# The first batch's length-47 steps: from one frequency at a time to chunks of four on 64x64 tiles, joined on GpSimd

## The chip, the cores and the metric

The kernel runs on one core of a Trainium2 chip. The metric is device time in microseconds (us) of one execution, as the median of several runs. A core has TensorE (PE in the profile, with weight loads as PEld), VectorE (DVE), ScalarE (ACT), GpSimd (POOL) and SyncE (SP); the last only issues DMAs here. ScalarE and GpSimd issue DMAs as well, each in the order of its own queue.

## The reference

All data are float32, but the mixer's weights arrive as float64. There are two parts in a row: a filter in the frequency domain along the sequence, and an MLP mixer over tokens and channels.

```python
batch, seq, dim = 8, 3008, 256
X = np.fft.rfft(x, axis=1)
F = (filt_r + 1j * filt_i)[None, :, :]       # 1505 x 256
y = np.fft.irfft(X * F, n=3008, axis=1)
# mixer on y: w_tok1 (3008, 256), w_tok2 (256, 3008), w_ch1 (256, 1536), w_ch2 (1536, 256)
h = np.maximum(y.transpose(0, 2, 1) @ w_tok1, 0) @ w_tok2
u = y + h.transpose(0, 2, 1)
out = u + np.maximum(u @ w_ch1, 0) @ w_ch2
```

## The kernel before

The transform of length 3008 is split into 64 x 47. For each batch the kernel does a step of length 64 (`a_unit` or `a_pair`), then, for each of 32 frequencies k2 of that step, a step of length 47 forward, the product with the filter, and a step of length 47 back. The results go to DRAM (`g_tmp`), and are read back in another layout (`t4_load`, L778) for the mixer, which undoes the length-64 step along with its own products. `dft(bs)` (L563) is a generator that issues these steps piece by piece; the main program steps through it and puts other work between the pieces. The order of instructions on each engine is thus written out by hand; nothing is reordered by a scheduler, and each engine runs its own list in order and waits on semaphores.

The first batch is a case by itself. The results of its length-64 step stay on the chip: they are copied into `turned` and transposed in place in 32x32 blocks (L650), so that the 4 x 24 rows of one frequency lie in four groups of 32 partitions, of which 24 are used. Then, one frequency k at a time:

- `b_unit(k)` (L663): one matmul of 128x128 weights on 256 columns, into PSUM, and one VectorE product with the filter (L670, 128x512).
- `bi_unit(k)` (L673): two matmuls (L679) that accumulate the two products, and a ScalarE copy out of PSUM (L689 in `by_block`). Every second frequency's results go to `g_tmp` in one DMA on ScalarE's queue (L686).

For this, the filter rows of two frequencies are loaded into the lower 64 partitions (`filt_load`, L235, mostly on GpSimd's queue, six DMAs a pair), ScalarE copies them to the upper 64 (`filt_double`, L253), and ScalarE makes a second, swapped and negated copy of the table of weights (`table_turn`, L260 and L261).

The other batches do the same in chunks c of four frequencies, on the four 64x64 quarters of TensorE: `b_sets(c)` (eight matmuls by `four`, L525), `products(c)` (two VectorE products of 128x1024, L706), `join(c)` (two VectorE additions of 128x512, L711 and L712) and `bi_sets(c)` (eight matmuls, L525). Their products lie in the tiles `p1` and `p2`, with one buffer each (pools `p1p`, `p2p`).

Beside the first batch's length-47 steps, the main program converts the mixer's float64 weights, 16 tiles over the 32 frequencies: `convert_middle` and `convert_end` take turns, one at each step of the generator. A tile takes an ACT scaling (L281), two VectorE instructions in the middle (L283, L284), two at the end (L287, L289), and, for the first 18 tiles, two TensorE matmuls on 512 columns (L327 on the first two's result, L328 on the last two's), which `convert_middle` issues in `sum_up`, and a ScalarE copy (L330). So the matmuls of a tile stand on TensorE behind the step in which the next `convert_middle` falls. After these steps come the rest of the weights, with the sums of GpSimd (`combine`, L380 to L384), the token mixing of the first batch (`token_sums`, L783), and then the loop over the mixer's items, `mix`, with the other batches' filter steps in it. Some GpSimd additions on the weights (L801, L922) run there too.

```python
for i, _ in enumerate(dft(GROUPS[0])):
    k = i - NXC - 2
    ...
        while half < 2 * IN_B * (k + 1) // K2:
            if half % 2:
                convert_end()
            else:
                convert_middle()
            half += 1
```

Of the kernel before, what the change touches and what calls it, by code (L numbers as in the profile page):

```python
# [10 lines left out]
FP32 = mybir.dt.float32  # L11
# [48 lines left out]
def _make_tables():  # L60
# [41 lines left out]
    wbi0 = np.zeros((4, K2, K2, P + KR))  # L102
    wbi0[:, 0:A, :, 0:P] = wb
    wbi0 = wbi0.reshape(P, K2, P + KR)
    wbi0[:, :, P:] = wi
    places = np.zeros((P, K2, 2 * P))
    places[:, :, 0::2] = wbi0[:, :, 0:P]
    places[:, :, TI:TI + 2 * KR:2] = wbi0[:, :, P:]
    wbi0 = np.concatenate((places[one, :, 0:P], places[two, :, P:]))
    wbi0 = wbi0.reshape(P, K2 // WC, WC, P).transpose(0, 1, 3, 2)  # L110
    wb = wb.reshape(KR, K2, P)
    wbi = np.zeros((P, K2 // KC, 4, HALF))
    for h in range(2):
        r, to = slice(h * HALF, h * HALF + KH), slice(h * HALF, (h + 1) * HALF)
        for i in range(KC):
            wbi[r, :, i] = wb[h * KH:(h + 1) * KH, i::KC, to]
            wbi[i * HALF:(i + 1) * HALF, :, 2 + h, 0:KH] = wi[to, i::KC, h * KH:(h + 1) * KH]
    wa = wa.reshape(P, K2, 4)
# [10 lines left out]
def kernel(  # L129
# [92 lines left out]
    def filt_quad(c):  # L222
        t = filts[c % FB]
        for i, src in enumerate((filt_r, filt_i)):
            for odd in range(KC):
                k, to = c * KD + odd, odd * HALF
                nc.sync.dma_start(t[to:to + A, i], raw(src, k, [[64 * D, A], [KC * D, 2], [1, D]]))
                down = t[to + 32:to + 32 + A]
                if k:
                    nc.sync.dma_start(down[0:A - 1, i], raw(src, 64 - k, [[64 * D, A - 1], [-KC * D, 2], [1, D]]))  # L230
                else:
                    nc.sync.dma_start(down[:, i, 0], raw(src, 32, [[64 * D, A], [1, D]]))
                    nc.sync.dma_start(down[0:A - 1, i, 1], raw(src, 64 - KC, [[64 * D, A - 1], [1, D]]))

    def filt_load(c):  # L235
        t, k0 = filts_0[c % len(filts_0)], c * KC


        q = nc.gpsimd if c != 1 else nc.sync
        for src, i, p0 in ((filt_r, 0, 0), (filt_i, 1, 0)):  # L240
            q.dma_start(t[p0:p0 + A, i], raw(src, k0, [[64 * D, A], [D, KC], [1, D]]))
            lo = p0 + 32
            if k0 == 0:
                q.dma_start(t[lo:lo + A, i, 0, :], raw(src, 32, [[64 * D, A], [1, D]]))
            k = max(k0, 1)

            for j0, n in ((0, 16), (16, A - 1 - 16)):
                q.dma_start(t[lo + j0:lo + j0 + n, i, k - k0:KC, :],
                            raw(src, 64 * (j0 + 1) - k, [[64 * D, n], [-D, k0 + KC - k], [1, D]]))

    def filt_double(c):
        t = filts_0[c % len(filts_0)]
        nc.scalar.copy(out=t[HALF:P], in_=t[0:HALF])  # L253


    turn_i = sp.tile([P, 4, WC, KR], FP32, tag="s", name="turn_i")

    def table_turn(g, wb):
        wi, to = wb[:, TI:TI + 2 * KR:2].rearrange("p r k -> p k r"), turn_i[:, g % 4]
        nc.scalar.copy(out=to[0:HALF], in_=wi[HALF:P])  # L260
        nc.scalar.activation(out=to[HALF:P], in_=wi[0:HALF], func=AF.Copy, scale=-1.0)  # L261


# [299 lines left out]
    def dft(bs):  # L563
# [5 lines left out]
        kept = []  # L569

        def table_load(c):
            if first:
                if c < 5:
                    where, tag = (t1p, "t1") if c > 2 else (wbp, "wb")
                    t = where.tile([P, 2 * P, WC], FP32, tag=tag, name="wb")
                    for h in range(2):
                        nc.gpsimd.memset(t[half_of(h), ts(1 - h, P)], 0.0)
                    kept.append(t)
                wbs[c] = kept[c % 5]
                for h in range(2):  # L580
                    nc.sync.dma_start(wbs[c][half_of(h), ts(h, P)], wbi0_d[half_of(h), c])
            else:
                wbs[c] = wbp.tile([P, 2, 4, HALF], FP32, tag="wb", name="wb")
                nc.sync.dma_start(wbs[c], wbi_d[:, ts(c, 2)])
# [4 lines left out]
        def w_load(c):  # L589
            table_load(c)  # L590
            (filt_load if first else filt_quad)(c)
# [45 lines left out]
        for i, u in enumerate(() if tiled else todo):  # L637
            if first and i in (0, 2):
                w_load(i // 2)
            if first and i in (6, 8):  # L640
                table_load(i // 2 - 1)
# [9 lines left out]
        t2s, t3s, prods = {}, {}, {}  # L651
# [11 lines left out]
        def b_unit(k):  # L663
            ps = bank("pg").rearrange("p (b d) -> p b d", b=2)[:, 0:nb, :]
            nc.tensor.matmul(ps, wbs[k // WC][:, 0:2 * P:2, k % WC], turned[:, k, :].unsqueeze(1), start=True, stop=True)  # L665
            t = filts_0[k // KC % len(filts_0)]
            if k == 0:
                prods["all"] = p1p.tile([P, 2, 2, D], FP32, tag="p1", name="p1")
            p1 = prods["all"][:, k % 2]
            nc.vector.tensor_tensor(out=p1, in0=ps.to_broadcast([P, 2, D]), in1=t[:, :, k % KC, :], op=ALU.mult)  # L670
            prods[k] = (p1[:, 0:1], p1[:, 1:2])

        def bi_unit(k):  # L673


# [692 lines left out]
```

## Time and profile before

| | |
|---|---|
| median of 3 runs | 2401.42 us (2400.28 to 2402.54) |
| profiled execution | 2401.9 us, span of the trace 2400.1 us |
| busy share of the span | PE 98%, PEld 84%, DVE 81%, ACT 29%, POOL 27% |
| length-64 step of the first batch | PE 5.0 to about 20.6 us, transposes on DVE to 31.1 us |
| length-47 steps of the first batch | first TensorE matmul 31.2 us, first product 32.5 us, last product 101.8 us |
| last store to `g_tmp` of the first batch | issued at 104.7 us |
| filter issues on GpSimd | 92 of about 0.56 us |

Times in the trace count from the span's start. A row of the stretches has its bounds, its length, then the busy time of PE, PEld, DVE, ACT and POOL with the number of instructions in brackets, the granted TensorE clock, the share of the DMA engines and GB/s. A row of the timeline has start, duration, engine, line, operation, output and inputs, and in square brackets how long the engine had been idle and who ended it. Matmuls overlap in the records: two float32 records of 256 columns show 0.59 us, but take 0.43 us of the chain. A chain row has start, duration and what ran.

### The profile page before, as it was taken

The numbers are of one execution on the slowest core, as the hardware profiler recorded it, in microseconds if no ns is written. First come the engines' busy times: TensorE is split into PE (matmuls) and PEld (weight loads), VectorE is DVE, ScalarE is ACT, GpSimd is POOL, SyncE is SP. The second block draws the span as 40 slices with busy tenths as digits, with TensorE's granted clock in tenths as the row PEclk, the third lists the DMA queues.
The fourth block names the chain that finished last, engine by engine and source line by source line (L and its number), as shares of the span: only waits on it lengthen the run. The fifth ranks groups of instructions, "written<-read, shape, count | busy, mean of one in ns | idle before, by whom it ended". The sixth has DMA issues, their size and how long they took to land.

```text
span 2400.1 us, 37049 instructions
## 1 busy us (share of the span) xinstructions
PE 2361.8 (98%) x13132; PEld 2012.4 (84%) x13132; DVE 1949.6 (81%) x3669; ACT 689.8 (29%) x1339; POOL 641.6 (27%) x1124
## 2 busy tenths in 40 slices
PE   7989999999999999999999999999999999999998
PEld 4767788888898888988888888988889888898887
DVE  7798887888887888778887788788887788877786
ACT  5732222222223222232222222122222322212222
POOL 7475624211211121112111311221121112112121
PEclk8999999999999999999999999999999999999999
DMA  8864446333353333533344333533335433331100
GB/s 224 241 190 127 155 127 217 121 106 92 113 173 129 101 99 108 197 111 99 98 150 155 113 94 103 189 117 107 92 114 172 134 96 99 108 130 32 39 14 21
DMA packets 190423, 294.28 MB, mean 123 GB/s; under 512 B 34444, under 2 KB 124962, under 8 KB 190238
## 3 DMA queue, kind: packets, MB, share of 16 engines
q1 hardware_dynamic: 148750, 231.24, 30.9%
q0 software_dynamic: 34688, 53.83, 8.5%
q10 hardware_dynamic: 6800, 6.85, 0.9%
q8 instruction: 104, 1.70, 0.3%
q14 instruction: 81, 0.66, 0.1%
HBM read 209.06 MB, written 82.72 MB: 122 GB/s over the span
## 4 chain that ended last, share of the span: by engine, by line
PE 91%; DVE 3%; DMA 3%; issue 1%; POOL 1%; ACT 0%; SPq 0%; DVEq 0%; ACTq 0%; POOLq 0%
PE ps_po L1008 35%; PE ps_pg L974 19%; PE ps_pg L990 15%; PE ps_b L525 3%; PE ps_b L838 3%; PE ps_acc L895 3%; PE ps_acc L838 2%; PE ps_b L895 2%; PE ps_pg L525 2%; PE ps_acc L873 2%; PE ps_b L873 2%; DMA st<-in_moe_w_tok_dram 1%; DVE t L952 1%; PE ps_pg L665 0%; PE ps_acc L881 0%
## 5 line engine op out<-in xcount | busy, mean ns | idle before, releaser
L1016 POOL DMA_DIRECT2D out_dram<-r x752 | 409.7, 553 | 1452.2 <-issue 790.6
L995 ACT ACTIVATE hh<-hh 128x512 f32<-128x512 f32 (+1 forms) x576 | 347.8, 621 | 1014.9 <-DVE hh L952 1011.0
L952 DVE TENSOR_TENSOR hh<-ps_pg,s 128x512 f32<-128x512 f32 (+3 forms) x864 | 482.2, 586 | 169.1 <-ACT s L977 158.9
L1008 PE MATMUL ps_po<-t,wc 128*128 128x256 f32 (+1 forms) x2296 | 558.2, 379 | 1.0 <-DVE t L952 0.9
L1008 PEld LDWEIGHTS ps_po<-t,wc 128*128 128x128 f32 x2296 | 426.7, 190 | 96.8 <-issue 38.3
L974 PE MATMUL ps_pg<-v,wc 128*128 128x256 f32 (+1 forms) x1728 | 413.2, 375 | 1.5 <-POOL wc L383 1.5
L1008 PE MATMUL ps_po<-hh,wc 128*128 128x256 f32 (+1 forms) x1722 | 412.6, 376 | 0.6 <-POOL wc L384 0.6
L974 PEld LDWEIGHTS ps_pg<-v,wc 128*128 128x128 f32 x1728 | 328.1, 190 | 39.8 <-POOL wc L383 2.3
L1008 PEld LDWEIGHTS ps_po<-hh,wc 128*128 128x128 f32 x1722 | 327.7, 191 | 38.8 <-POOL wc L384 1.4
L990 PE MATMUL ps_pg<-u,wc 128*128 128x256 f32 (+1 forms) x1152 | 291.7, 376 | 2.2 <-DVE hh L952 2.1
L952 DVE TENSOR_TENSOR t<-t,hh 128x256 f32<-128x256 f32 (+1 forms) x576 | 246.9, 429 | 19.8
L990 PEld LDWEIGHTS ps_pg<-u,wc 128*128 128x128 f32 x1152 | 217.0, 190 | 33.6 <-DVE hh L952 7.3
L952 DVE TENSOR_TENSOR s<-ps_pg,hh 128x512 f32<-128x512 f32 (+1 forms) x288 | 196.0, 681 | 30.0
L977 ACT COPY s<-ps_pg 128x256 f32<-128x256 f32 (+1 forms) x288 | 106.0, 368 | 331.9 <-PE ps_pg L974 328.6
L952 DVE TENSOR_TENSOR t<-hh 128x512 f32<-128x512 f32 (+1 forms) x288 | 194.2, 674 | 0.6 <-ACT hh L995 0.6
L974 PE MATMUL ps_pg<-u,wc 128*128 128x256 f32 (+1 forms) x576 | 169.6, 376 | 3.7 <-DVE hh L952 3.7
L990 PE MATMUL ps_pg<-v,wc 128*128 128x256 f32 (+1 forms) x576 | 168.8, 375 | 0.0
L974 PEld LDWEIGHTS ps_pg<-u,wc 128*128 128x128 f32 x576 | 108.0, 190 | 20.0 <-DVE hh L952 7.9
L990 PEld LDWEIGHTS ps_pg<-v,wc 128*128 128x128 f32 x576 | 108.9, 190 | 12.9
L952 DVE TENSOR_TENSOR u<-ps_acc,u 128x256 f32<-128x256 f32 (+1 forms) x84 | 46.2, 550 | 72.5 <-PE ps_acc L895 50.1
L952 DVE TENSOR_TENSOR u<-ps_b,u 128x512 f32<-128x512 f32 (+2 forms) x126 | 74.5, 591 | 28.8 <-PE ps_b L895 26.7
L895 PE MATMUL ps_acc<-w 128*128 128x256 f32 (+1 forms) x336 | 85.2, 376 | 0.0
(164 smaller groups left out, 2688.9 us busy)
## 6 DMA issues: line engine op xcount, KB each, us to landing
w<-w_tmp SPq DMA_DIRECT2D x84, 448.0 KB
w<-w_tmp SPq DMA_DIRECT2D x35, 896.0 KB
out_dram<-r POOLq DMA_DIRECT2D x696, 32.0 KB, 3.5
g_tmp<-t SPq DMA_DIRECT2D x112, 192.0 KB
t<-g_tmp SPq DMA_DIRECT2D x42, 512.0 KB
t<-z_tmp SPq DMA_DIRECT2D x196, 96.0 KB
z_tmp<-t SPq DMA_DIRECT2D x72, 256.0 KB
wb<-wbi_t SPq DMA_DIRECT2D x56, 256.0 KB
```

The source lines that it names most:

```text
L525: nc.tensor.matmul(outs(i, j), stat(i, j), mov(i, j), start=True, stop=True)
L838: nc.tensor.matmul(ps[:, at], w[:, n], mov, start=(j == 0 and i in (0, 2)), stop=(j == AP - 1 and i >= 5))
L873: nc.tensor.matmul(ps[:, ds(q * P, n)], t4[b, c][:, r, ts(dh, P)], wai[:, 0:n], start=(first and q == 0), stop=(not first and q == 3))
L895: nc.tensor.matmul(ps[:, ds(j * hw, hw)], h1[:, n, :], w2m[m % 2][:, at, 0:hw], start=(i < 2 and j == 0), stop=(j == len(todo) - 1))
L952: nc.vector.tensor_tensor(out=out, in0=in0, in1=in1, op=op)
L974: nc.tensor.matmul(ps[:, 0:hw], chan[0][:, jp, n, :], mov, start=True, stop=True)
L977: nc.scalar.copy(out=s[:, 0], in_=g[0][:, 0, 0:hw])
L990: nc.tensor.matmul(ps[:, 0:hw], chan[0][:, jp, n, :], mov, start=True, stop=True)
L995: nc.scalar.activation(out=hs, in_=hs, func=AF.Relu)
L1008: nc.tensor.matmul(po[i][:, j, 0:hw], chan[1][:, jp, n, :], mov, start=(jp == 0 and first == 1), stop=(jp == JP - 1 and last == 1))
L1016: q.dma_start(bass.AP(tensor=ob.tensor, offset=ob.offset + row * D + g * cw, ap=[[N1 * D, 32], [D if h else -D, n], [1, cw]]), blocks[ts(g ...
```

## The change

The first batch's length-47 steps take the form of the other batches' chunks. `b_unit`, `bi_unit`, `filt_load`, `filt_double` and `table_turn` go. `b_sets` reads `turned` instead of a tile loaded from DRAM, with 64 rows of a group pair where the others have 48, and a table `wbi0` of its own with zeros in the unused rows. `join` runs on GpSimd for this batch. The stores to `g_tmp` are two DMAs for four frequencies, on ScalarE's queue. The filter is loaded by `filt_quad` into all 128 partitions, its real part from GpSimd's queue and its imaginary part from SyncE's (the first chunk's from GpSimd's alone), into five buffers; the two extra ones are zeroed whole. The generator gives four steps a chunk, so the conversions keep their places, one half tile to a step. The banks of PSUM are `acc` and `b` for `b_sets` and the two `pg` for `bi_sets`.

```diff
+    wbi0 = wbi.copy()
+    wbi0[:, :, 0:KC] = 0.0
+    for g in range(4):
+        wbi0[g * K2:g * K2 + A, :, 0:KC] = wbi[g // 2 * HALF + g % 2 * A:][0:A, :, 0:KC]
...
-    def filt_quad(c):
-        t = filts[c % FB]
-        for i, src in enumerate((filt_r, filt_i)):
+    def filt_quad(c, bufs=None, queues=(nc.sync, nc.sync)):
+        t = (bufs or filts)[c % len(bufs or filts)]
+        for i, (src, q) in enumerate(zip((filt_r, filt_i), queues)):
             for odd in range(KC):
                 k, to = c * KD + odd, odd * HALF
-                nc.sync.dma_start(t[to:to + A, i], raw(src, k, [[64 * D, A], [KC * D, 2], [1, D]]))
+                q.dma_start(t[to:to + A, i], raw(src, k, [[64 * D, A], [KC * D, 2], [1, D]]))
...
         def w_load(c):
             table_load(c)
-            (filt_load if first else filt_quad)(c)
+            filt_quad(c, *((filts_0, (nc.gpsimd, nc.sync if c else nc.gpsimd)) if first else ()))
...
         def b_sets(c):
-            pss, wb, t2 = two_banks(turn), wbs[c], t2s[c]
+            pss, wb = two_banks(turn), wbs[c]
+            t2, n = (turned[:, ts(c, KD)], HALF) if first else (t2s[c], KH)
             for j in range(2):
-                four(lambda h, i: pss[h][half_of(i), j], lambda h, i: wb[half_of(h, KH), j, i],
-                     lambda h, i: t2[half_of(h, KH), j * KC + i])
+                four(lambda h, i: pss[h][half_of(i), j], lambda h, i: wb[half_of(h, n), j, i],
+                     lambda h, i: t2[half_of(h, n), j * KC + i])
             return pss
...
-        def join(c):
+        def join(c, q=nc.vector):
             p1, p2 = prods[c, 0], prods.pop((c, 1))
-            nc.vector.tensor_tensor(out=p1[:, 0], in0=p1[:, 0], in1=p2[:, 1], op=ALU.subtract)
-            nc.vector.tensor_tensor(out=p1[:, 1], in0=p1[:, 1], in1=p2[:, 0], op=ALU.add)
+            q.tensor_tensor(out=p1[:, 0], in0=p1[:, 0], in1=p2[:, 1], op=ALU.subtract)
+            q.tensor_tensor(out=p1[:, 1], in0=p1[:, 1], in1=p2[:, 0], op=ALU.add)
...
-        for k in range(K2 + 1):
-            if k < K2:
-                b_unit(k)
...
+        for i in range(2):
+            t = t2p.tile([P, 2, KC, D], FP32, tag="t2", name="filt")
+            nc.gpsimd.memset(t, 0.0)
+            filts_0.append(t)
+        for c in range(2, 4):
+            filt_quad(c, filts_0, (nc.gpsimd, nc.sync))
+        for c in range(last):
+            pss = b_sets(c)
+            if c:
+                bi_sets(c - 1, ("pg", "pg"))
+            products(c, pss)
             yield
+            join(c, nc.gpsimd)
+            if c + 4 < last:
+                filt_quad(c + 4, filts_0, (nc.gpsimd, nc.sync))
+            yield
+            if 1 <= c < last - 2:
+                table_load(c + 2)
+            yield
+            yield
+        bi_sets(last - 1, ("pg", "pg"))
+        yield
```

## The prediction

> **What bounds the kernel now.** I read the page first, then busy time by stretch, then the chain of waits over the stage that the change touches, then single instructions. The page says that TensorE (PE) ends almost everything; the changed steps run from 32.5 to 105 us.
>
> ```profile
> PE 2361.8 (98%) x13132; PEld 2012.4 (84%) x13132; DVE 1949.6 (81%) x3669; ACT 689.8 (29%) x1339; POOL 641.6 (27%) x1124
> ```
>
> Inside the stage two rows of the stretches (bounds, length, busy us of PE, PEld, DVE, ACT, POOL, then granted clock, DMA share, GB/s) show PE full, ScalarE (ACT) at 90% and VectorE (DVE) at 75 to 80%:
>
> ```profile
> 50.00:60.00 10.00, 10.00 (x38) 7.33 (x37) 7.34 (x14) 9.03 (x16) 8.18 (x15) 1.00 0.81 239
> 60.00:70.00 10.00, 10.00 (x37) 7.40 (x36) 8.00 (x15) 9.03 (x17) 8.94 (x18) 1.00 0.78 224
> ```
>
> The chain over the same stretch (start, us, what) holds PE and nothing else:
>
> ```profile
> 50.68 0.86 PE ps_po L327 x2
> 51.54 0.86 PE ps_po L328 x2
> 52.40 0.45 PE ps_pg L665 x2
> 52.85 0.86 PE ps_b L679 x4
> 53.71 0.46 PE ps_pg L665 x2
> 54.17 0.86 PE ps_acc L679 x4
> 55.04 0.86 PE ps_po L327 x2
> ```
>
> From one L327 to the next is 4.36 us: two frequencies (2 x 0.45 + 2 x 0.86) and one weight tile on PE (0.86 + 0.86). Four frequencies, which the new code makes one chunk, cost 8.72 us in this steady part. Over the whole stage the first product starts at 32.51, the last at 101.81: 69.30 / 31 x 4 = 8.94 us. The last store to DRAM is issued at 104.7, so the stage takes 72.2 us. What comes behind waits for it: the weight loads on GpSimd's (POOL's) queue stand behind its last reads of g_tmp, which begin at 108.25. A shift of the stage's end passes on whole.
>
> **Part by part.** *PE.* Other batches already run the new form: L525 shows 16 records in 0.93 us (chain, 285.16). A chunk then costs PE two such groups, 1.9 us, beside two weight tiles, 3.45: 5.35 for 8.72. *ACT* loses L253 (16 x 1.04) and L260/L261 (32 x 0.55), 34.3 us, and has 16 copies of 128x512 at 0.59 for 32 at 0.36. It isn't late in either form. *Queues.* POOL gives up about 92 filter issues of 0.56 (51 us) for 38 (21 us) and takes 16 additions; in a chunk that is two joins, four issues and a weight load, 2 x 1.6 + 4 x 0.56 + 0.57 = 6.0 us, less than any pitch below. What stands behind a join there (filter rows four chunks ahead, weights five tiles ahead) has time. SP's added filter loads wait for products that are done chunks before their use. Tables, filters and results move as many bytes as before. I cost these at nothing; without the cover of four chunks a late landing would cost its 3.5 us.
>
> *The new cycle.* `prods` has one buffer for p1 (p1p), so the products of a chunk wait for the previous chunk's second matmuls, and those for the join. PE's order in a chunk is b_sets, bi_sets of the chunk before, one weight tile, then a second one that VectorE finishes only after this chunk's products; b_sets of the next chunk stands behind it. So the pitch is a sum along one path:
>
> ```profile
> 284.98 1.04 PE L525 MATMUL ps_pg<-p,wb 64*64 64x256 f32 x16
> 286.12 1.23 DVE L706 TENSOR_TENSOR p<-ps_b,filt 128x1024 f32<-128x1024 f32 x1 [0.33 <-PE ps_pg L525]
> 287.26 1.22 DVE L706 TENSOR_TENSOR p<-ps_acc,filt 128x1024 f32<-128x1024 f32 x1
> 288.45 0.42 DVE L952 TENSOR_TENSOR hh<-ps_pg,s 128x256 f32<-128x256 f32 x1
> ```
>
> Two products: 286.12 to the next instruction at 288.45, 2.33 us. The conversion L283, L284, L287, L289 by the starts in the stage: 0.45 + 0.61 + 0.45, and 0.69 for the last, 2.20. Hand-over to PE 0.08, L328 0.86. Then b_sets and bi_sets, from the first L525 at 284.07 to the product at 286.12, 2.05. Sum 7.52 us, if the join costs nothing. VectorE alone has 2.33 + 2 x 2.15 = 6.63, so it isn't the bound.
>
> *The join on GpSimd.* An addition of 128x128 takes 0.455 us at least, 128x384 0.995 (L384, L801): 0.27 a step, so 1.27 for 128x512; the 128x384 mean of 1.109 puts it at 1.4. Both joins start when the second product ends, just as VectorE begins that conversion. Here is what such a meeting does, the same join on VectorE alone and then beside two GpSimd additions:
>
> ```profile
> 225.90 0.68 DVE L711 TENSOR_TENSOR p<-p,p 128x512 f32<-128x512 f32 x1
> 226.49 0.68 DVE L712 TENSOR_TENSOR p<-p,p 128x512 f32<-128x512 f32 x1
> ...
> 245.25 1.23 DVE L711 TENSOR_TENSOR p<-p,p 128x512 f32<-128x512 f32 x1
> 246.40 1.48 DVE L712 TENSOR_TENSOR p<-p,p 128x512 f32<-128x512 f32 x1
> ```
>
> ```profile
> 244.91 2.43 POOL L801 TENSOR_TENSOR w<-w 128x384 f32<-128x384 f32 x2
> ```
>
> Alone the pair takes 1.27 us, beside GpSimd 2.63: 1.36 lost to two additions of 384. For 512, 1.36 x 4/3 = 1.8 us a chunk. The conversions themselves were slowed too: from 144.20 to 147.03 the four took 2.83 beside about five additions of 128, 0.63 lost; eight such widths make 1.0. I take 1.8, from the row with long additions, and keep 0.9 to 2.2. It lies before L289's end, on the path: pitch 9.3 us for 8.72.
> The Trainium skill's page "SBUF — State Buffer" (Who interferes with whom) speaks against the join: a VectorE instruction with two SBUF inputs and a GpSimd one that reads SBUF shut each other out for the whole instruction. The rows agree in kind; by the rule taken fully the loss would be an estimated 2.5 us a chunk and the sum below 6 us higher.
>
> *Stage.* PE starts at 31.2 as now; with 16 records at half clock the first product comes at 33.1 instead of 32.5. Seven pitches of 9.3 reach 98.3. The last chunk: 2.33 + 2.20 + 1.8 + 0.08 + 0.86 + 0.95 to bi_sets' end, two copies 1.07, an issue 0.31: 9.7, so 108.0 for 104.7. That is +3.3 us.
>
> *The clock.* PE would work 5.35 of 9.3 us. Its pause from the end of the first weight tile (1.75 us into the chunk) to L284's end (2.33 + 1.14 + about 0.9 = 4.4) is 2.6 us, followed after 0.86 of work by another of 1.1. What the trace shows of pauses (stretches again):
>
> ```profile
> 138.00:142.00 4.00, 2.50 (x7) 0.97 (x7) 3.86 (x7) 1.76 (x3) 3.65 (x8) 1.00 0.92 276
> ...
> 146.00:150.00 4.00, 1.89 (x7) 1.14 (x7) 3.90 (x7) 1.60 (x3) 3.76 (x7) 0.99 0.64 209
> 150.00:153.20 3.20, 3.20 (x9) 2.49 (x9) 3.06 (x6) 1.04 (x3) 3.09 (x7) 0.50 0.60 204
> ```
>
> After a pause of 1.5 us (140.2 to 141.7) the clock stayed at 1.00; after one of 2.1 (146.3 to 148.4) it was 0.50 for 3.4 us. Each chunk has a longer one. At half clock L328 and both groups cost up to 2.76 us more a chunk, or nothing where the drop passes during the pause; the drop falls between pause and groups, so I take a third, 0.9, times 8 = 7 us, with 0 and 22 as ends. (A gain is excluded: no slower clock shortens PE's work.)
> The skill's page "TensorE: Matmul & The Clock Gate" (HAM oscillation) asks only for no idle gaps over about 3.4 us; by that nothing drops here and the sum stays at +3.3. The row at 150 us, after a 2.1 us pause, decides against it.
>
> Together +10 us. The profiled execution took 2401.9 us (span 2400.1), the median is 2401.4; on the median that is 2411.5.
>
> **The rivals.**
> 1. *No contention that matters (faster).* GpSimd's additions slip between VectorE's instructions. Pitch 7.52: 33.1 + 7 x 7.52 + 7.9 = 93.6, 11 us earlier, 2390.5; with the clock dropping at times (the pause is still 1.7 us) about -5, 2396. For it: the path's other terms are all measured, ACT and PE are relieved. Against: the 1.36 us above, and the stage's bytes, 239 GB/s at a DMA share of 0.81 now, would need 284 where 279 was the most seen. Without a drop of the clock it decides where the loss is under 0.8 us a chunk ((11.1 - 4.8) / 8); at 1.4 (11.1 / 8) it comes out level.
> 2. *Contention, clock holds.* +3.3 us, with 0.9 to 2.2 of loss -4 to +6.5: 2404.7, mostly no measurable change. For it: VectorE-bound stretches at 160 to 190 us kept 1.00. Against: those have pauses under 1 us.
> 3. *The clock is low nearly throughout.* +3.3 + 22 = +25, 2426.7. For it: the pause recurs in every chunk. Against: at half clock PE would work 10.7 us a chunk without pause, which released it at 153.3.
> 4. *The stage isn't what ends last.* Then nothing moves. Against: the chain above is PE of these steps alone, and the reads of g_tmp follow it.
>
> **How the numbers follow.** What a measurement of this kernel can tell from no change is 0.2%, 4.8 us. My forecast, +6 to +16 (the clock's share from 3 to 13), 0.45; rival 1 0.21; rival 2 0.20; rival 3 0.12; rival 4 0.02. Faster: most of rival 1 (0.18) and 0.02 of rival 2. Same: 0.13 of rival 2, 0.03 of rival 1 and rival 4: 0.18. Slower: the rest, 0.62. Cases of both signs hold chance, so the likeliest one's own range is 2407.5 to 2417.5; the whole one leaves out the lower part of rival 1 and half of rival 3: 2394 to 2423.
>
> **What would show it.** Right: products of the first batch (128x1024) some 9.3 us or more apart; conversions just behind them stretched from 2.2 to about 4 us beside GpSimd additions of 1.3 to 1.6; the granted clock under 1.00 in stretches of the stage; the last store near 108 to 115 us. Wrong: a pitch near 7.5 with conversions of 2.2 us; a clock of 1.00 throughout (then +3.3 only); waits for filter or table DMAs ahead of the products, which would be a cause I cost at nothing; or a stage that ends later and a run that doesn't.

## The result, and the profile after

| | before | after |
|---|---|---|
| median | 2401.44 us (2400.28 to 2402.54, 4 runs) | 2425.89 us (2420.89 to 2426.96, 4 runs) |
| ratio | | 1.0098, 95% interval 1.008 to 1.0115 |
| profiled execution (span) | 2401.9 us (2400.1) | 2426.4 us (2424.6) |
| first and last product of the stage | 32.5, 101.8 us | 33.2, 117.5 us (a chunk of four frequencies now has two products; the first of the two is given) |
| last store to `g_tmp` issued | 104.7 us | 127.5 us |
| token product of the first batch starts | 110.2 us | 134.1 us |

The change costs 24.5 us, 14.4 more than the forecast and above its range. All but 0.7 us of it arises before 134.1 us, in the stage that the change touches: 23.8 us there. In the kernel after, the products stand in L637 (L706 before), the join in L642 and L643, the conversion in L246 (ScalarE) and L248, L249, L252, L254 (VectorE), the weight tile's matmuls in L292 and L293, the weight loads in L310, the tables in L537, the filter in L222 and L225, the stores in L654.

The stretches of after, from product to product (bounds, length, busy us of PE, PEld, DVE, ACT, POOL, then granted clock, DMA share, GB/s):

```profile
44.34:56.72 12.38, 8.84 (x41) 3.23 (x41) 9.54 (x10) 0.95 (x2) 6.24 (x6) 0.72 0.47 134
56.72:68.98 12.26, 7.47 (x41) 2.93 (x41) 7.32 (x11) 3.16 (x6) 5.78 (x6) 0.86 0.61 180
...
81.64:94.03 12.39, 8.72 (x41) 3.25 (x41) 8.54 (x10) 3.38 (x7) 4.01 (x4) 0.72 0.82 252
94.03:105.39 11.36, 7.78 (x41) 2.90 (x42) 8.54 (x11) 3.31 (x7) 3.98 (x4) 0.85 0.73 222
```

No engine is full, and the clock, 0.97 in the mean of this stage before, is 0.72 to 0.86. One chunk takes 12.05 us in the mean (33.17 to 117.51, seven chunks), for 8.94 before and 9.3 in the forecast (10.2 with its clock term). One chunk of after in the timeline, VectorE first, then GpSimd, then TensorE:

```profile
82.78 1.21 DVE L637 TENSOR_TENSOR p<-ps_b,filt 128x1024 f32<-128x1024 f32 x1
83.91 0.41 DVE L248 TENSOR_SCALAR both<-both 128x512 uint32<-128x512 uint32 x1
84.36 1.63 DVE L249 SCALAR_TENSOR_TENSOR both<-st,both 128x512 uint32<-128x512 uint32 x1
86.03 1.38 DVE L252 TENSOR_SCALAR both<-both 128x512 uint32<-128x512 uint32 x1
87.44 0.69 DVE L254 SCALAR_TENSOR_TENSOR both<-st,both 128x512 f32<-128x512 uint32 x1
...
88.51 0.69 DVE L249 SCALAR_TENSOR_TENSOR both<-st,both 128x512 uint32<-128x512 uint32 x1
89.23 0.43 DVE L252 TENSOR_SCALAR both<-both 128x512 uint32<-128x512 uint32 x1
```
```profile
84.17 1.27 POOL L642 TENSOR_TENSOR p<-p,p 128x512 f32<-128x512 f32 x1 [5.67 <-DVE p L637]
85.41 1.71 POOL L643 TENSOR_TENSOR p<-p,p 128x512 f32<-128x512 f32 x1
```
```profile
86.05 1.12 PE L292 MATMUL ps_po<-both,wai_t 128*128 128x512 f32 x2 [2.65 <-DVE both L249]
88.19 2.07 PE L293 MATMUL ps_po<-both,wai_t 128*128 128x512 f32 x2 [1.02 <-DVE both L254]
...
91.95 1.93 PE L490 MATMUL ps_pg<-p,wb 64*64 64x256 f32 x16
```

The conversion from 83.91 takes 4.2 us for the 2.2 that the prediction read from the stage before: L249 takes 1.63 and L252 1.38 while GpSimd joins, 0.69 and 0.43 in the next conversion, when it doesn't. That is 1.9 us together. Then TensorE, after pauses of 2.65 and 1.02 us, runs at half speed: the pair of L293 shows 2.07 where the pair of L292, of the same shape, showed 1.12 two microseconds before, and one group of 16 takes 1.93 for 1.04 in the kernel before.

Early in the stage there is something else. The first row below is before, the second after, both the same 12 us:

```profile
37.00:49.00 12.00, 12.00 (x45) 8.74 (x44) 8.87 (x16) 9.80 (x18) 8.88 (x16) 0.99 0.79 213
```
```profile
37.00:49.00 12.00, 8.71 (x41) 3.30 (x42) 10.37 (x12) 2.23 (x4) 7.09 (x7) 0.76 0.27 78
```

The DMA engines are busy 0.27 of the time for 0.79, and bring 78 GB/s for 213: about 1.6 MB less in these 12 us. From 30 to 110 us it is 186 GB/s for 235. SyncE's own queue in after shows why:

```profile
37.13 0.30 SPq L222 DMA_DIRECT2D filt<-in_filt_i_dram  x1
...
39.43 1.78 SPq L222 DMA_DIRECT2D filt<-in_filt_i_dram  x1
41.25 0.33 SPq L225 DMA_DIRECT2D filt<-in_filt_i_dram  x1
41.76 2.09 SPq L222 DMA_DIRECT2D filt<-in_filt_i_dram  x1
...
46.70 3.78 SPq L310 DMA_DIRECT2D st<-in_moe_w_tok_dram  x4
```

From 37.13 to 46.65 it issues nothing but twelve filter loads of 46 to 48 KB, and four weight loads of 256 KB stand behind them. What then waits for what is in the timeline of ScalarE and the chain of after:

```profile
57.19 3.62 ACTq L654 DMA_DIRECT2D g_tmp<-t  x2
60.85 0.59 ACT L295 COPY w<-ps_po 128x512 f32<-128x512 f32 x1 [15.56 <-DMA filt<-in_filt_i_dram]
```
```profile
49.87 8.12 DMA st<-in_moe_w_tok_dram
...
58.05 3.25 DMA wb<-wbi_t
```

The results that L654 stores were ready at 45.3, yet ScalarE issued the store at 57.19 and, but for the two issues, did nothing in the 15.56 us before 60.85. A table was requested at 58.05, right when a weight load that has nothing to do with it landed (49.87 + 8.12 = 57.99). In the program every DMA of SyncE's and ScalarE's queues takes the next of eight semaphores in turn, and waits until the DMA that had it before has landed (in the trace the issues of the two queues carry eight semaphores in turn, and each waits on its own): at most eight are under way on the two queues together. The kernel after has eleven such DMAs per chunk in this part (four weight loads, four filter loads, two stores, a table).

So there were two candidates: the pace of the engines (the contention of VectorE and GpSimd, and the clock), and the supply by the queues.

### The profile page after: what moved, and what is told of

It is laid out like the page before. It is cut to its first block, busy times and chain, and to the rows that moved or that the text cites. A ratio compares the mean times of both kernels' runs of the same rounds, so it can differ in the third digit from the quotient of the medians.

```text
span 2424.6 us, 36935 instructions
## 1 busy us (share of the span) xinstructions
PE 2354.7 (97%) x13196; PEld 1983.7 (82%) x13196; DVE 1964.8 (81%) x3653; ACT 652.7 (27%) x1275; POOL 639.7 (26%) x1076
## 4 chain that ended last, share of the span: by engine, by line
PE 89%; DVE 5%; DMA 3%; issue 1%; POOL 1%; SPq 1%; ACT 0%; DVEq 0%; ACTq 0%; POOLq 0%
PE ps_po L938 34%; PE ps_pg L904 19%; PE ps_pg L920 15%; PE ps_b L490 3%; PE ps_b L768 3%; PE ps_acc L825 3%; PE ps_acc L768 2%; PE ps_pg L490 2%; PE ps_b L825 2%; PE ps_acc L803 2%; PE ps_b L803 2%; DMA filt<-in_filt_i_dram 1%; DVE t L882 1%; DVE both L249 1%; DVE hh L882 1%
## 5 line engine op out<-in xcount | busy, mean ns | idle before, releaser
L920 PEld LDWEIGHTS ps_pg<-u,wc 128*128 128x128 f32 x1152 | 217.0, 190 | 33.2 <-DVE hh L882 6.9
L882 DVE TENSOR_TENSOR s<-ps_pg,hh 128x512 f32<-128x512 f32 (+1 forms) x288 | 196.1, 681 | 32.5 <-DVE hh L882 3.2
L882 DVE TENSOR_TENSOR u<-ps_b,u 128x512 f32<-128x512 f32 (+2 forms) x126 | 74.4, 591 | 28.9 <-PE ps_b L825 26.7
L637 DVE TENSOR_TENSOR p<-ps_acc,filt 128x1024 f32<-128x1024 f32 x64 | 77.7, 1214 | 20.5 <-PE ps_pg L490 17.0
```

The costliest lines, as they stand in the source:

```text
L637: nc.vector.tensor_tensor(out=prods[c, h], in0=pss[h].unsqueeze(1).to_broadcast([P, 2, 2, D]), in1=bufs[c % len(bufs)], op=ALU.mult)
L882: nc.vector.tensor_tensor(out=out, in0=in0, in1=in1, op=op)
L920: nc.tensor.matmul(ps[:, 0:hw], chan[0][:, jp, n, :], mov, start=True, stop=True)
```

## The experiments

Each version is compared with the kernel before on the same chip. The table sums them up: where the time goes is read from the start of the first chunk's products to that of the fifth's ("first four chunks", in which the weight tiles come from SyncE) and from the fifth's to the eighth's ("last three"). The "dummies" are two extra matmuls per chunk whose results nobody uses.

| version | filter's 2nd half | first four | last three | time, us |
|---|---|---|---|---|
| after | SyncE | 48.5 | 35.9 | 2425.9 |
| e1 join on VectorE | SyncE | 57.7 | 31.6 | 2428.5 |
| e2 dummies | SyncE | 49.7 | 28.9 | 2421.2 |
| e4 early first product | SyncE | 52.6 | 29.7 | 2426.3 |
| e7 stores | SyncE | 49.9 | 35.9 | 2424.6 |
| e8 stores, table | SyncE | 47.8 | 30.1 | 2421.7 |
| e11 dummies, stores | SyncE | 46.7 | 28.9 | 2420.2 |
| e15 dummies, stores, table | SyncE | 42.3 | 30.8 | 2418.9 |
| e16 the same, join on VectorE | SyncE | 50.3 | 26.3 | 2419.7 |
| e17 as e16 | GpSimd | 36.1 | 26.8 | 2405.2 |
| e19 as e17, no dummies | GpSimd | 45.5 | 29.0 | 2414.3 |
| e20 after, join on VectorE | GpSimd | 43.1 | 30.9 | 2412.5 |
| e3 after | GpSimd | 55.8 | 35.9 | 2433.9 |
| e10 all levers | GpSimd | 34.9 | 33.1 | 2410.9 |
| e13 memset | GpSimd | 35.4 | 29.1 | 2405.0 |
| e14 no join | GpSimd | 33.2 | 30.9 | 2406.8 |
| e18 five tables | GpSimd | 33.1 | 23.6 | 2406.0 |
| e21 last stores ScalarE | GpSimd | 32.6 | 22.8 | 2403.5 |
| e22 last stores GpSimd | GpSimd | 31.1 | 30.9 | 2404.8 |

### One lever at a time

**The join on VectorE (e1)** takes the contention away.

```diff
-            join(c, nc.gpsimd)
+            join(c)
```


> The changed kernel with the first batch's join on VectorE instead of GpSimd. Theory A (GpSimd and VectorE shut each other out, and TensorE's pauses lower its clock while it stands on the path): the 1.9 us that the conversion loses beside the join go, two additions of 0.6 us come onto VectorE's path, so 0.7 us less a chunk, 5 to 6 us in all; the pauses stay and the clock still drops: about 2420 us. Theory B (the added filter loads on SyncE's queue and the waits of ScalarE for its DMA semaphores set the pitch): nothing is gained, 2426, or 8 x 1.2 = 10 us lost, up to 2436.

2428.47 us, ratio 1.0111 (1.0096 to 1.0126). L249 is back at 0.69 and the other chunks are 8.8 to 11.5 us long, but one takes 27.4 (54.43 to 81.85): TensorE waits 15.2 us for a table, and ScalarE's stores are issued up to 9.3 us long. What the contention had cost was paid at another place; the time is theory B's.

**Two dummy products per chunk (e2)** in TensorE's long pause hold the clock.

```diff
             yield
+            for _ in range(2):
+                nc.tensor.matmul(pss[0].rearrange("p j d -> p (j d)"), wai_t, ...)
             join(c, nc.gpsimd)
```


> The changed kernel with two extra 128x128 matmuls on 512 columns (1.7 us at full clock) after the first weight tile of each chunk, into a bank that is free there; their results are not used. Theory A: the pause of about 2.6 us shrinks to about 1, the granted clock stays at 1.00 after the start, the second weight tile and both groups take 2.8 us instead of up to 5.5, the pitch falls from 12.05 to 9.4 to 10 us: 2405 us (2403 to 2412). Theory B: TensorE's speed is not what waits; no change, 2426, or slower.

2421.21 us, 1.0079 (1.0064 to 1.0094): 4.7 us less than after. Six of the seven chunks take 9.5 to 10.7 us at a clock of 0.95 to 1.00 in five of them, one takes 19.6. The time lies between the two theories. The second and the third chunk:

```profile
42.97:52.67 9.70, 7.76 (x45) 3.15 (x45) 9.49 (x10) 0.95 (x2) 6.24 (x6) 1.00 0.46 131
52.67:72.30 19.63, 11.10 (x45) 4.57 (x45) 6.74 (x11) 3.16 (x6) 5.78 (x6) 0.68 0.61 167
```

So the clock costs 12.05 - 9.7 = 2.35 us in a chunk to which nothing comes late, and the long chunk takes most of it back.

**The filter on GpSimd's queue alone (e3)**, with the join still on GpSimd.

```diff
-            filt_quad(c, filts_0, (nc.gpsimd, nc.sync))
+            filt_quad(c, filts_0, (nc.gpsimd, nc.gpsimd))
```
(the same for the loads of chunk 1 and of chunk c + 4)

> The changed kernel with both halves of the first batch's filter on GpSimd's queue. Theory A: the 5.2 us that VectorE waits for scaled weights in the third and fourth chunk go, but the conversion then meets the join in these chunks too (2 x 1.9), so little changes: 2422 to 2427 us. Theory B: SyncE's queue and ScalarE's semaphores are free, the pitch falls by at least the 5.2 us and the late waits behind them: 2410 to 2418.

2433.9 us, 1.0133 (1.0118 to 1.0148), slower than after. The first chunk takes 19.2 us: the join stands on GpSimd behind the issues of the filter, and TensorE's weight load waits 8.1 us for it. So the time doesn't tell what the filter's queue costs. But the chunks behind the first do tell something: no filter load stands on SyncE's queue there, TensorE waits for no DMA, each chunk's products start some 0.15 us after TensorE's last group, and the chunks still take 11.4 to 12.9 us, 12.1 in the mean, as in after. Two of them, the second at a DMA share of 0.26:

```profile
65.40:77.79 12.39, 8.72 (x41) 3.26 (x41) 9.59 (x10) 3.39 (x7) 10.85 (x12) 0.73 0.58 159
77.79:89.15 11.36, 7.83 (x41) 3.00 (x42) 9.60 (x11) 3.40 (x7) 8.82 (x10) 0.85 0.26 63
```

So contention and clock set this pace by themselves.

**The first tables' product one step earlier (e4)**, ahead of the second weight tile.

```diff
             yield
+            pss = b_sets(c + 1)
             if 1 <= c < last - 2:
```


> The changed kernel with the next chunk's first group of matmuls (b_sets) issued one step after the products, ahead of the second weight tile, where TensorE pauses; the rest as it is. Theory A: 0.95 us (1.9 at half clock) leaves the path and the pauses become shorter than about 1 us, so the clock holds: pitch 2.33 + 4.1 + 0.08 + 0.86 + 1.1 = 8.5 us, 2398 to 2406 us. Without the clock's part (pauses irrelevant, clock as low as now): pitch 10, 2410. Theory B: no change, 2426.

2426.33 us, 1.0101 (1.0084 to 1.0118). Five of seven chunks fall to 8.7 to 9.7 us, one takes 23.6 (TensorE waits 14.7 us in it for a table). The time is theory B's. Three shortenings (e1, e2, e4), and each time one long chunk between 52 and 82 us took most of the gain back or more.

### The stores and the tables

**The stores on SyncE's queue (e7)**, so that ScalarE isn't held.

```diff
-                (nc.scalar if first else nc.sync).dma_start(g_d[...]
+                nc.sync.dma_start(g_d[...]
```


> One edit to the kernel after: the stores of this stage's results are issued on SyncE's queue instead of ScalarE's. Theory Q (ScalarE, which also converts the raw weights, stands behind its own stores: it issued the first at 57.19 although the rows were there at 45.29, and the last weight load it needs is consumed late because of that): the waits of VectorE for L246 (2.95 and 2.29 us in the third and fourth chunk) go, ScalarE has no idle time over 4 us behind a store, products still start 11 to 12 us apart for the clock and the contention, and the time is 2419 to 2423. Theory L (the loads themselves land late, 8 us and more after their issue with at most eight under way on the two hardware queues, so a free ScalarE finds nothing to convert): the waits stay where they are under the name of a DMA (st or wb), and the time is 2425 to 2428.

2424.57 us (1.0079 to 1.0109). ScalarE's 15.56 us are gone, VectorE no longer waits for L246, and nothing is gained that the intervals could tell: the chunks take 11.3 to 13.6 us, and the time lies between the two theories. Theory Q's waits weren't what set the end.

**The table ahead of the filter loads as well (e8).**

```diff
                 bi_sets(c - 1, ("pg", "pg"))
+            if 1 <= c < last - 2:
+                table_load(c + 2)
             products(c, pss)
```


> As the kernel with the stores on SyncE's queue, and the table of the chunk after next is requested right behind the second tables' product, ahead of the filter loads of four chunks later, instead of behind them and two weight tiles. Theory Q: the table was never late by itself; within 1.5 us of the kernel with the stores moved alone. Theory L: the table is what stood behind SyncE's filter loads (requested at 58.05 and landed 8.12 us later in the kernel after), the waits of TensorE for wb go, and the time falls by a further 3 to 6 us below the kernel with the stores moved alone, to 2414 to 2420.

2421.71 us (1.0064 to 1.0095), 2.9 below the version before it with overlapping intervals, so the two can't be told apart.

**Dummies and stores together (e11).**

```diff
+                nc.tensor.matmul(pss[0]..., wai_t, ...)        # as e2, twice
+                nc.sync.dma_start(g_d[...]                     # as e7
```

> The two dummy products per chunk that held the clock at 1.00 (2421.21 us with one chunk 19.6 us long, the others 9.7), together with the stores on SyncE's queue. The dummy products are no part of the computation's result. Theory Q: the long chunk shrinks to 9.7 as the others, the stage ends some 10 us earlier than with the dummies alone, and the time is 2409 to 2413, which is where the forecast without its clock term lay. Theory L: the long chunk stays at 17 to 20 with the wait named after a DMA (st or wb) and the time is 2418 to 2422.

2420.18 us (1.0059 to 1.0093), as theory L had it: the long chunk is still 16.9 us, with 5.4 of TensorE's wait for a table.

**Dummies, stores and tables together (e15).**

```diff
+                nc.tensor.matmul(pss[0]..., wai_t, ...)        # as e2, twice
+                nc.sync.dma_start(g_d[...]                     # as e7
+                table_load(c + 2)                              # as e8
```

> Join still on GpSimd; the stores on SyncE's queue, the table requested ahead of the filter loads, and the two dummy products per chunk that hold the clock (no part of the result). Theory S (three causes that add: 8 chunks slowed by the clock, one late table or weight, and the contention that the forecast had): every chunk takes 9.6 to 9.8, no chunk over 11, the last product starts at 100 to 103 and the time is 2410 to 2414, 12 to 15 below the kernel after. Theory L (memory cannot bring the weights at this pitch): one chunk of 15 us or more remains and the time stays at 2417 to 2421.

2418.94 us (1.0054 to 1.0085). Three chunks of 9.7, then 13.2 and 11.6; ScalarE now waits for weight tiles (8.1, 8.9, 7.7 us). Theory S falls; the time is theory L's, though no chunk takes 15 us. The chunks of 9.7 show the pace with the join on GpSimd, the clock held and nothing late:

```profile
43.19:52.90 9.71, 7.77 (x45) 3.15 (x45) 9.51 (x11) 2.72 (x5) 6.25 (x6) 1.00 0.46 129
```

**The same with the join on VectorE (e16).**

```diff
-            join(c, nc.gpsimd)
+            join(c)
```

> The kernel with the dummy products, the stores on SyncE's queue and the early table, and the join on VectorE as well, so that GpSimd does not hold VectorE up. Theory S: the 1.9 us per chunk that the contention costs (L249 1.63 for 0.69, L252 1.37 for 0.42) go, VectorE pays 1.28 for the join that it now does, which lies in part beside the path, and the chunks take 8.4 to 9.0: the time is 5 to 9 below the kernel with the join on GpSimd, 2403 to 2408. If the contention was no cost on the path, the two agree within 2 us.

2419.65 us (1.0061 to 1.0088): no gain, with the contention gone and the clock held outside the long chunks. The last three chunks are 8.7 to 8.8 us each, 0.9 less than the 9.7 with the join on GpSimd; two of the first four are 15.9. In them ScalarE waits for weights, as its timeline shows:

```profile
59.80 0.66 ACT L246 ACTIVATE both<-st 128x512 f32<-128x512 f32 x1 [9.40 <-DMA st<-in_moe_w_tok_dram]
...
76.83 0.66 ACT L246 ACTIVATE both<-st 128x512 f32<-128x512 f32 x1 [13.88 <-DMA st<-in_moe_w_tok_dram]
```

### The split of the filter

**The last version with the filter back on one queue (e17)** and nothing else (the memset of the last weight tile goes from GpSimd to VectorE, so that SyncE doesn't wait for GpSimd there).

```diff
-                filt_quad(c + 4, filts_0, (nc.gpsimd, nc.sync))
+                filt_quad(c + 4, filts_0, (nc.gpsimd, nc.gpsimd))
...
-            nc.gpsimd.memset(st.bitcast(U32)[:, 512:1024], 0)
+            nc.vector.memset(st.bitcast(U32)[:, 512:1024], 0)
```


> The kernel with dummy products, stores on SyncE, early table and join on VectorE (2419.65, two chunks of 15.9 us), with both halves of the filter on GpSimd's queue again, and the memset of the last weight tile on VectorE (no other edit; the dummies are no part of the result). Theory F (the filter's second half on SyncE's queue waits for the products and holds up the weight tiles behind it): the waits of ScalarE for weight tiles in the chunks from 51.8 to 83.6 go, the chunks take 8.6 to 9.2, the last product starts at 94 to 98 instead of 109.9, and the time is 2404 to 2408. Theory M (the memory brings the weights no faster, whatever the queue): chunks of 12 us and more remain in that stretch and the time is 2413 to 2419.

2405.18 us, 1.0013 (1.0004 to 1.0023): 14.5 us less by this edit (14.1, each taken from the kernel before on its own chip). The memset's move has no part in that: in e16 it was done at 58.83, and the loads into that tile were issued from 87.30 on. The stretch that had 0.27 now has

```profile
37.00:49.00 12.00, 10.50 (x50) 3.98 (x48) 11.44 (x18) 3.41 (x6) 11.25 (x14) 0.96 0.95 232
```

and from 36 to 72 us ScalarE waits for no weight tile. SyncE issues eight weight loads from 27.85 to 41.23, where after issued four and then the twelve filter loads. Theory F holds. Whether the filter loads do their harm by their place in SyncE's order or by taking four of the eight semaphores a chunk was not separated.

**The same without the dummies (e19).**

```diff
-                nc.tensor.matmul(pss[0].rearrange("p j d -> p (j d)"), wai_t, ...)
```

> As the kernel with the filter back on GpSimd's queue, but without the dummy products: the clock is left to itself. If the clock's cost is independent of the queues (the first pair of runs gave 2.35 us per chunk, 12.05 to 9.7), the chunks take 10.5 to 11.5 and the time is 2417 to 2424, 13 to 18 above the kernel with dummies. If the clock falls only where TensorE pauses for long (the join on VectorE and no late load leave pauses of 1.5 to 2 us instead of 2.6 and more), it holds most of the time, the chunks take 9 to 9.5 and the time is 2407 to 2411.

2414.33 us, 1.0048 (1.0035 to 1.0062): the clock costs 9.2 us when the queues are mended, between the two expectations. Chunks with a clock of 0.99 and 1.00 take 8.6 and 8.8 us, those with 0.71 and 0.72 take 11.5 and 12.2:

```profile
66.26:78.44 12.18, 8.73 (x41) 3.26 (x41) 8.90 (x14) 3.38 (x7) 9.37 (x13) 0.72 0.86 212
78.44:87.28 8.84, 6.08 (x41) 2.42 (x42) 7.77 (x12) 3.33 (x7) 0.00 (x0) 1.00 0.80 299
```

**The kernel after with the join on VectorE and the filter on one queue (e20)**, stores and tables left as they were.

```diff
-            join(c, nc.gpsimd)
+            join(c)
-                filt_quad(c + 4, filts_0, (nc.gpsimd, nc.sync))
+                filt_quad(c + 4, filts_0, (nc.gpsimd, nc.gpsimd))
-            nc.gpsimd.memset(st.bitcast(U32)[:, 512:1024], 0)
+            nc.vector.memset(st.bitcast(U32)[:, 512:1024], 0)
```

> The kernel after with the join on VectorE (2428.47, one chunk of 27 us) and both halves of the filter on GpSimd's queue, the memset on VectorE; the stores stay on ScalarE's queue and the table stays where it was. Theory F: the 27-us chunk goes, because the weight tiles are there and because ScalarE's stores then wait for loads issued long before; 2408 to 2416, above the kernel with all levers by what the first product's earlier place and the clock bring. If ScalarE's stores are a cause of their own (they share eight completion slots with SyncE's loads), ScalarE still stands 5 us and more behind a store in several chunks and the time is 2418 to 2426.

2412.54 us, 1.0045 (1.0031 to 1.0058): 15.9 us less than with the split (e1; 16.2, each taken from its own kernel before), and not above the version with stores and tables moved as well (2414.33; the intervals overlap). ScalarE no longer stands behind a store for 5 us or more. Its blocked store was a consequence of the split, not a cause beside it.

### Is there a version that beats the kernel before

**All levers but the dummies (e10)**: join on VectorE, first product early, stores on SyncE, table early, filter on GpSimd's queue.

```diff
+            pss = b_sets(c + 1)                                # as e4
+                nc.sync.dma_start(g_d[...]                     # as e7
+                table_load(c + 2)                              # as e8
+            join(c)
+                filt_quad(c + 4, filts_0, (nc.gpsimd, nc.gpsimd))
```

> All levers but the dummies: join on VectorE, first tables' product one step earlier, stores on SyncE's queue, table requested early, filter of chunks 2 to 7 all on GpSimd's queue (SyncE's and ScalarE's queues then carry 7 DMAs per chunk instead of 11). Theory Q: with ScalarE and SyncE free, VectorE's own work (2.33 of products, 2.20 of conversion, 1.1 to 1.4 of join) and TensorE's set a pitch of 7.5 to 8.5 us, the last product starts near 90 instead of 117.5, and the time is 2394 to 2400. Theory L: the weight loads still come no faster than the memory gives them, the pitch stays at 10 or more in the first five chunks, and the time is 2408 to 2416. If GpSimd's queue is too slow for eight filter loads per chunk (1.0 us of issue each), products wait for filter rows and the pitch is 9 to 10 throughout.

2410.9 us, 1.0036 (1.0023 to 1.0049). Four chunks of 8.4 to 9.0, then one of 10.1 and one of 15.25: SyncE issued one load of the last weight tile at 62.13 and the other only at 74.77, behind a memset that GpSimd did at 74.03. The time is theory L's, the pace of the first chunks isn't: it is near theory Q's.

**The memset on VectorE (e13).**

```diff
-            nc.gpsimd.memset(st.bitcast(U32)[:, 512:1024], 0)
+            nc.vector.memset(st.bitcast(U32)[:, 512:1024], 0)
```

> The kernel with all levers (2410.9) had one chunk of 15.25 us: SyncE's queue stood from 62.13 to 75.36 before the last weight tile, which waits for a memset that GpSimd reaches at 74.03, behind its filter issues. Here that memset is done by VectorE, and nothing else is changed. Theory S: the chunk shrinks to 8.4 to 9.0, SyncE issues the table for the chunk after without that wait, and the time is 2403 to 2406. Theory L: the memory is the limit of that chunk (300 GB/s in it), the wait moves to another load, and the time is 2408 to 2411.

2405.0 us, 1.0016 (1.0007 to 1.0025), as theory S had it; a chunk of 12.75 is left at the end.

**No join (e14)**: TensorE takes both halves (`bi_sets_4`, 16 matmuls for 8), with a negated copy of the table by ScalarE.

```diff
-            join(c)
+            negate(c)
...
+                stat = neg[half_of(i), c % 3, j] if last_of and h == 0 else wb[half_of(i), j, 2 + h]
+                mov = p2[half_of(i), 1 - h, j] if last_of else p1[half_of(i), h, j]
+                nc.tensor.matmul(pss[i][half_of(h), j], stat, mov, start=not last_of, stop=bool(last_of))
```


> As the kernel with all levers and the memset on VectorE, and no join at all: TensorE takes both halves of the products in turn, with 16 small products more per chunk and a negated copy of a quarter of the table that ScalarE writes (128x128 per chunk). VectorE's work falls from 8.3 to about 7.0 us per chunk. Theory S (VectorE's work is now the pitch): chunks take 7.0 to 7.8, the last product starts at 83 to 88, and the time is 2391 to 2398, below the kernel before. Theory L (the DMA engines were busy 0.86 to 1.08 of the time at a pitch of 8.4 to 9): loads land late, the pitch stays at 8.4 or more and the time is 2401 to 2406.

2406.81 us, 1.002 (1.0011 to 1.0029). After the first, chunks of 7.3 to 8.4 us, and one of 16.2 in which TensorE waits for a table. The time is just above theory L's; the gain of a faster chunk came back as a wait.

**Two more table buffers (e18).**

```diff
+            where, tag = (t1p, "t1") if first and c % 5 > 2 else (wbp, "wb")
-            if 1 <= c < last - 2:
-                table_load(c + 2)
+            if c and c + 4 < last:
+                table_load(c + 4)
```

> The join-free version (2406.81; chunks 7.3 to 8.4 but one of 16.2, in which TensorE waits 6.7 us for a table requested at 76.59) with two more table buffers, so that each table is requested four chunks ahead. Theory T (that table was late in its place): the long chunk falls to 8 to 10, and the time is 2397 to 2401, level with the kernel before or under it. Theory M (by then the DMA engines are full, 276 GB/s at 0.97 in that chunk, and whatever is asked for last is late): another load is waited for in its place, and the time stays within 3 us of 2406.8.

2405.95 us, 1.0015 (1.0006 to 1.0024). The long chunk is gone, as theory T had it, but the time is theory M's. The last chunk's products start at 89.05, yet the token products start at 114.78, later than the 110.24 of before. SyncE's queue in this version:

```profile
88.04 14.72 SPq L734 DMA_DIRECT2D t<-g_tmp  x5
102.86 0.85 SPq L676 DMA_DIRECT2D g_tmp<-t  x2
```

The store of a late chunk stands 14.72 us behind loads of earlier results.

**The last three chunks' stores on ScalarE's queue (e21).**

```diff
-                nc.sync.dma_start(g_d[0][...]
+                (nc.scalar if c > 4 else nc.sync).dma_start(g_d[0][...]
```

> The join-free version with five table buffers (2405.95), the stores of chunks 5 to 7 on ScalarE's queue. Theory O (order on SyncE: the stores stood 15 us behind loads of earlier results): the last store is issued at 98 to 101 instead of 109.13, the token products start at 104 to 108 instead of 114.78, and the time is 2396 to 2401, under the kernel before. Theory M (memory: 259 GB/s at 0.92 between 80 and 100; the later loads come no sooner): the token products start after 111 and the time stays at 2403 to 2406.

2403.49 us, 1.0006 (0.9998 to 1.0015): level with before, and theory M's time; the token products start at 110.88.

**Or on GpSimd's (e22).**

```diff
-                (nc.scalar if c > 4 else nc.sync).dma_start(g_d[0][...]
+                (nc.gpsimd if c > 4 else nc.sync).dma_start(g_d[0][...]
```

> The same with the stores of chunks 5 to 7 on GpSimd's queue, where the second weights' loads stand ahead of them (one of them waited 8.89 us for a free buffer). Theory O: 2397 to 2403, equal to the version with ScalarE's queue or up to 3 us above it. Theory M: 2403 to 2407, as with ScalarE's.

2404.82 us, 1.0012 (1.0003 to 1.0021), theory M's time, with the token products at 117.26. No version beats the kernel before. The one that comes level moves 232 GB/s at a DMA share of 0.89 from 30 to 110 us; before moves 235 at 0.86. That the memory's rate is the floor there fits this, but was not tried by itself (by taking bytes away). Against a plain limit of that height stands the row of e19 above: 299 GB/s at a share of 0.80 for 8.84 us.

## Why the prediction was wrong

**The bound of before.** Right: the stage ends the run, and its end passed on whole. Rival 4 fell with that. TensorE was full, and the prediction used the column beside it only against rival 1: the DMA engines were at 0.72 to 0.97 in stretches of 12 us from 37 to 97 us, and no version brought more bytes from 30 to 110 us. (Its words "279 was the most seen" hold for the stage; the same trace has 300 GB/s from 290 to 300 us.) That there was little to win, and that a delayed load costs at once, fits this.

**The path of a chunk.** Right in form: products, conversion, L293, two groups. In the chunk from 81.64 the products take 2.27 (2.33 forecast), the conversion 4.2 (4.0).

**The join on GpSimd.** Right: 1.9 us for the 1.8 forecast, in L249 and L252. Of GpSimd's two additions the first took its forecast 1.27 while L249 lost 0.94, the second 1.71. What the join's place costs a chunk when nothing else is late and the clock is at 1.00 is less, 0.9 us (9.7 in e15, 8.8 in e16), since VectorE then does the join itself. In the program's time no run shows it (e15 and e16 are 0.7 apart). The Trainium skill's "SBUF — State Buffer" (Who interferes with whom) has the two engines shut each other out for a whole instruction; the rows agree in kind (L249 0.94 longer, L252 0.95), and the loss stays below the 2.5 us estimated from it.

**The clock: mis-sized.** The prediction took a third of 2.76 us, 0.9. In that chunk L293 took 1.9 (88.19 to 90.1) for 0.86 and the two groups 3.8 for 2.05: 2.8 us, the whole of it. The drop doesn't fall "between pause and groups"; it has fallen by the time L293 starts and lasts through both groups. Of the seven chunks four have a clock of 0.72 or 0.73 and only two 0.85 or 0.86 (the first, at 0.57, still has the low clock in which the stage starts). The runs give the price: with the join on GpSimd and nothing late, a chunk takes 12.1 us with the clock left to itself (e3) and 9.7 with it held (e2, e15). That is 2.4 us a chunk where the sum had 0.9, on a pitch of 9.7 where it had 9.3. With 12.1 for 10.2, eight chunks are 15 us more, and the miss is 14.4. In e19 the drop came at shorter pauses still: from 87.28 to 98.82 it had 1.65 and 1.14 us of them and a clock of 0.71. The skill's "TensorE: Matmul & The Clock Gate" (HAM oscillation) asks for no gap over about 3.4 us; here pauses of 2.65 and 1.02 us in a chunk were enough, and the measurement decides.

**The queues: costed at nothing.** Rival 3 (the clock low nearly throughout) had 2426.7, and 2425.9 was measured. Its clock is near what the rows show, but that it meets the time so closely is partly luck, for it left out a second cause: with the clock held only 4.7 us came back (e2). The prediction had named the cover of four chunks for the filter, and looked at the wrong loads: the filter rows are in time, but what stands behind them on SyncE's queue, weight tiles and tables, has no such cover. Twelve loads of 46 to 48 KB kept SyncE from 37.13 to 46.65, and the DMA share of that stretch fell to 0.27.

Either cause is enough for such a pace by itself. Contention and clock give 12.1 us a chunk without the split (e3); the split gives 12.6 in the mean of the first four chunks with the join on VectorE and the dummies in (e16, 50.3 us), where e17, without the split, takes 36.1. Taking one away uncovers the other, which is why no single edit gained over 5 us. Undone from the good end, each step has a price, every version taken from the kernel before on its own chip: the new form with all mended (e17) 3.5 above before; the clock let go (e19) +9.2; stores and tables as in the change (e20) -1.8; the filter split (e1) +16.2; the join put on GpSimd (after) -2.6. The steps add up to the 24.5 by construction, and the prices hold for this order only: the split, for one, costs so much with the join on VectorE. At -1.8 and -2.6 the intervals overlap, so these two are not told from nothing; that the last one is no loss fits VectorE's having time there while weights are late.

Rival 1 (no contention) and rival 2 (clock holds) fell by the rows above; rival 2's number, 2404.7, is near what the new form costs with the clock held and the filter on one queue (e17, 2405.2), but by luck in part: e17 also has the join on VectorE and the stores and tables moved.

## What to carry to other kernels

- When loads move to another queue, list what stands behind them there and how far ahead it is; a load that itself has time can still hold up one that hasn't. Where queues share a set of semaphores in turn, count the DMAs per round against their number.
- If several single edits leave the time in a narrow band and only move the longest wait, look for two bounds of equal height: mend everything first, then undo one thing at a time, and look in the runs for rounds that only one of the bounds can have set.
- Read the DMA share beside the busy engine. In this stage, whose DMA share was 0.86 already, none of the versions with faster engine work came below the kernel before.

## What was not expected of the hardware

- The clock fell for pauses of this kind: chunks with TensorE pauses of about 2.6 and 1.0 us alternated between full and half speed, at a mean of 0.72 to 0.85; two products more in the longer pause held it at 1.00, with pauses of 0.93 and 1.01 left.
- A small filter load's issue on SyncE showed 0.23 to 0.5 us mostly, but 1.8 to 2.1 us for three of the twelve from 37.13 to 46.65. Whether that is the queue or the memory was not tried.
